# Bucketed attention and two MLPs on one core: the product with v queued behind later scores, and low parts of q and V computed by GpSimd

## The chip, the cores and the metric

The kernel runs on one core of a Trainium2 chip. The metric is device time in microseconds (us) of a whole execution: the three timed runs of the kernel before took 835.03, 836.65 and 831.97 us, a median of 835.03. One further execution was recorded by the hardware profiler.

Names of the engines: PE is TensorE's matmul, PEld its weight load, DVE is VectorE, ACT ScalarE, POOL GpSimd. SP is SyncE, which here only issues DMAs; its queue stands in the trace as SPq. L448 is line 448 of the kernel.

## The reference

For 2 x 8 heads of 768 tokens with 64 numbers each, attention is computed among tokens of the same bucket alone. The bucket is the sign pattern of six projections of the token:

```
q_bits = einsum('bhsd,dk->bhsk', q, proj) > 0          # the same for k
mask   = bucket(q_bits)[:, :, :, None] == bucket(k_bits)[:, :, None, :]
scores = where(mask, q @ k.T / sqrt(64), -1e9)
attn   = exp(scores - max(scores)); attn = attn / (sum(attn) + 1e-9)
x      = (attn @ v), heads side by side: 1536 x 512
h = x @ w_in;   x = (h * sigmoid(1.702 h)) @ w_out     # first MLP, 512 -> 2048 -> 512
h = x @ w_in2;  x = (h * sigmoid(h)) @ w_out2          # second MLP, the same sizes
```

q, k, v and proj are float32; the weights of the MLPs arrive as float64 and are turned into float32 pairs on the chip.

## The kernel before

**Precision by pairs.** TensorE multiplies rounded numbers, so an operand is kept as a high part (rounded) and a low part (what the rounding left), and a product is made of three or so matmuls. The helper `natural` (L287) makes the two parts of q and k: VectorE writes the high part, and a subtraction (L293) gives the low part. Which engine does the subtraction is chosen by `LOWG`, one string for each batch: an operand named there goes to GpSimd, others to VectorE. In the first batch only k is named (and only from the third head on); in the second, k, q and v. V has the same split in `v_high` (L381, ScalarE scales V by a power of two and rounds it to f16) and `v_low` (L385): either one VectorE operation that scales and subtracts (L392), or ScalarE scales V in place (L389) and GpSimd subtracts (L390).

**A step of attention.** A step is 128 queries of one head against its 768 keys. A head has six steps, a batch of eight heads 48, both batches 96. In a step:
- `scores` (L395): four matmuls into PSUM, the bucket mask included by way of extra rows in BQ and BK. Two score buffers exist.
- `top` (L419, VectorE, L422): moves the scores out of PSUM and takes the extreme of each row; `exps` (L425, ScalarE, L427): the exponential.
- `p_high` (L430): the high part in f16, by ScalarE (L438) or VectorE (L436); `p_low` (L440, L442): the low part by GpSimd.
- `p_turn` (L444, L448): one DMA transpose, issued by SyncE, turns the parts of two steps. Two buffers `pt` receive it, so the transpose of a pair waits until the product of the pair before the last has read its buffer.
- `av` (L451): 18 matmuls (L460 to L462) of the transposed exponentials with V; `norm` (L465) divides and puts the result into the MLP's input when a group of steps is done.

Beside the steps, `ahead` (L498) prepares the next pair of heads in twelve slots, one for each step: loads of q, k and v (SyncE, each into a single buffer that is free once the low part has been computed from it), splits, turns on TensorE, copies into BQ and BK, and the bucket bits, whose rows SyncE copies into BQ and BK (`rows`, L342).

**Order of the work.** The program is a loop over steps (L559): in turn i of the first batch it emits `scores(i + 2)`, then `av(i - LAG)` with LAG = 3, `top(i + 1)`, `norm`, `ahead`, `exps(i)`, `p_high(i)`, `p_low(i)` and the transpose of the step before. A planner then simulates the engines and puts each engine's instructions into a queue, by readiness and by priority; the place in the program is the priority, moved forward for some tasks by the offsets in `SOONER`. On the chip each queue runs strictly in order. `tc.issue_after(x)` adds an order to that queue: what is emitted under it comes behind x on x's engine. It is no semaphore.

**The rest.** At turn `SWITCH - 1`, the last of the first batch's loop, the first MLP of the first batch starts and shares the engines with the attention of the second batch. The MLP of the second batch and the whole second MLP follow from about 415 us on. The weights are loaded, split on VectorE, ScalarE and GpSimd (L170 to L178) and partly spilled to HBM and read again.

Of the kernel before, what the change touches and what calls it, by code (L numbers as in the profile page):

```python
# [21 lines left out]
def tile_lsh_attention_two_mlps(  # L22
# [13 lines left out]
    V, A, G, T, SP = nc.vector, nc.scalar, nc.gpsimd, nc.tensor, nc.sync  # L36

    B, H, S, D = q.shape
# [4 lines left out]
    NC = S // P  # L43
    HS = S // 2
    HC = NC // 2
    HEADS = B * H
# [13 lines left out]
    QSCALE = -1.0 / math.sqrt(D)  # L60
    assert math.frexp(QSCALE)[0] == -0.5
    NBUF = 3
    LAG = 3
    TUL = 1
    MORE = {'aq': 1, 'ak': 1, 'p': 1, 'hl': 1, 'pt': 0}
    PTB = 2
    EARLY = 0
    WSTART = 38
    WEVERY = 3
    LOWG = ('k', 'kqv')  # L70
    COPY = ('k', 'q')
    FB = 2
    PB = 2
# [5 lines left out]

    SOONER = ({'ahead': 100, 'move': 20, 'load_v': 400, 'evict': 200, 'p_high': 200, 'natural': 800, 'p_turn': 35, 'turn': 100, 'p_low': 75, 'top': 35, 'exps': 75, 'bits': 300, 'norm': 35, 'load': 50, 'signs': 20}, {'scores': 200, 'evict': 50, 'norm': 300, 'av': 400, 'natural': 200, 'gate': 50, 'p_turn': 20, 'load_v': 200, 'load': 20, 'sum': 150, 'move': 20, 'p_high': 150, 'rows': 100, 'p_low': 75, 'bits': 100, 'exps': 20}, {'gate': 300, 'sum': 10, 'weights': 50})  # L80
    RATE = (3.4, 2.85)
    SWITCH = HEADS // 2 * NC + LAG + 1
    RING = 3
    RING2 = 6

# [2 lines left out]
    def sooner(task):  # L88
        n = SOONER[stage[0]].get(task, 0)
        return tc.high_priority(offset=n) if n else nullcontext()  # L90
# [158 lines left out]
    def attention(sp, s1, ps_m, ps_v, ahead_of, setup):  # L249
        nat, st = {}, {}  # L250
# [12 lines left out]
        N = len(steps)  # L263
# [23 lines left out]
        def natural(n, nm):  # L287
            x = nat[n, nm]
            hp, lp = (1, 0) if nm == "q" else (0, 1)
            E = G if nm in LOWG[stage[0]] and n > 1 else V  # L290
            t = sp.tile([P, NC, 2, D], F32R, tag="s" + nm, name="s" + nm, bufs=1)
# [27 lines left out]
        def place(n):  # L319
            return n % (NBUF + 1) if n < H else (n - H) % NBUF  # L320
# [64 lines left out]
        def v_low(pr, j):  # L385
            vs, s = st["v", pr]
            x = nat[pr, "v"][:, j]
            if "v" in LOWG[stage[0]]:
                A.activation(x, x, AF.Copy, scale=s[:, j:j + 1])  # L389
# [5 lines left out]
        def scores(j):  # L395
            n, c = steps[j]
            aq, ak = st["q", n], st["k", n]
            bq, bk = BQ[place(n)], BK[place(n)]
            ps = ahead_of["pool"].tile([P, 2, 512], F32, tag="s", name="pss")
            lq = aq.rearrange("p a b -> p (a b)")[:, c * P:(c + 1) * P]  # L400
            bq = bq[:, c * P:(c + 1) * P]
            for half in range(2):
                o = ps[:, half, 0:HS]
                T.matmul(o, lhsT=lq, rhs=ak[:, half, :], start=True, stop=False)  # L404
                T.matmul(o, lhsT=bq, rhs=bk[:, half * HS:(half + 1) * HS], start=False, stop=True)  # L405
            st["S", j] = ps[:, :, 0:HS]

        count = {}
# [42 lines left out]
        def av(j):  # L451
            (n, c), g = steps[j], group[j]
            vs, s = st["v", n // 2]
            pt = st.pop(("pt", j))
            if j == g[0]:
                st["av", g] = ps_v.tile([P, 512], F32, tag="av", name="pav")
            o = st["av", g][:, c * (D + 1):(c + 1) * (D + 1)]
            for i in range(NC):
                hv, lv = vs[:, n % 2, i, 0:D + 1], vs[:, n % 2, i, D + 1:]
                T.matmul(o, lhsT=pt[:, i], rhs=hv, start=(i == 0), stop=False)  # L460
                T.matmul(o[:, 0:D], lhsT=pt[:, i], rhs=lv, start=False, stop=False)
                T.matmul(o, lhsT=pt[:, NC + i], rhs=hv, start=False, stop=(i == NC - 1))  # L462


        def norm(g):  # L465
            n, c0 = steps[g[0]]
            m = len(g)
            pr, j = divmod(n, 2)
            vs, s = st["v", pr]
            y = st.pop(("av", g))[:, 0:NC * (D + 1)].rearrange("p (c d) -> p c d", c=NC)[:, c0:c0 + m]  # L470
            ri = sp.tile([P, NC, 1], F32, tag="ri", name="ri", bufs=1)[:, 0:m]
            V.tensor_scalar(ri, y[:, :, D:D + 1], EPS, s[:, j:j + 1], op0=ALU.add, op1=ALU.mult)
            V.reciprocal(ri, ri)
            if ("x", pr) not in st:
                st["x", pr] = sp.tile([P, NC, 2, D], F32, tag="xn", name="xn", bufs=1)
            V.tensor_tensor(out=st["x", pr][:, c0:c0 + m, j, :], in0=y[:, :, 0:D],
                            in1=ri.to_broadcast([P, m, D]), op=ALU.mult)
            if j == 1:
                halves = range(c0 // HC, (c0 + m) // HC)
                for half in halves:  # L480
                    x_turn(pr, half)
                for half in halves:
                    x_split(pr, half)
# [14 lines left out]
        def ahead(pr, s):  # L498
            a, b = 2 * pr, 2 * pr + 1
            return {  # L500
                -4: [(natural, a, "k")],
                -3: [(turn, a, "k", 0), (load, b, "k")],
                -2: [(evict, a, "k", 0), (turn, a, "k", 1), (natural, a, "q")],
                -1: [(evict, a, "k", 1), (turn, a, "q", 0), (v_max, pr), (load, b, "q")],
                0: [(evict, a, "q", 0), (turn, a, "q", 1), (natural, b, "k"), (move, a, "k")],
                1: [(evict, a, "q", 1), (turn, b, "k", 0), (load, a + 2, "k")],
                2: [(turn, b, "k", 1), (v_spread, pr), (natural, b, "q"), (move, a, "q")],
                3: [(evict, b, "k", 0), (evict, b, "k", 1), (turn, b, "q", 0), (v_scale, pr), (load, a + 2, "q")],
                4: [(evict, b, "q", 0), (turn, b, "q", 1), (v_high, pr, 0), (move, b, "k")],
                5: [(evict, b, "q", 1), (bits, pr, 0), (v_low, pr, 0)],  # L510
                6: [(signs, pr, 0), (bits, pr, 1), (v_high, pr, 1), (move, b, "q")],
                7: [(signs, pr, 1), (rows, pr), (v_low, pr, 1)],
                8: [(load_v, pr + 1)],
            }.get(s, [])

        def run(fs):
            for f, *a in fs:
                with sooner(f.__name__):
                    f(*a)
# [36 lines left out]
            run(ahead(1, s))  # L556


        for lead, first, last in ((2, 0, N // 2), (1, N // 2, N)):  # L559
            def at(f, j):  # L560
                if first <= j < last:
                    with sooner(f.__name__):
                        f(j)

            for i in range(first - lead, last + LAG + 1):
                if lead == 2:
                    at(scores, i + 2)
                at(av, i - LAG)
                at(top, i + lead - 1)
                m = i - LAG  # L570
                if first <= m < last and m == group[m][-1]:
                    with sooner("norm"):
                        norm(group[m])
                m = i - 2 * (2 - lead)
                if first <= m < last:
                    pr, s = divmod(m, 2 * NC)
                    with sooner("ahead"):
                        if pr + 1 < HEADS // 2:
                            run(ahead(pr + 1, s))
                        if s >= 2 * NC - 4 and pr + 2 < HEADS // 2:  # L580
                            run(ahead(pr + 2, s - 2 * NC))
                at(exps, i)
                at(p_high, i)
                at(p_low, i)
                at(p_turn, i - TUL)
                yield i
                if lead == 1:
                    at(scores, i + 1)
# [107 lines left out]
    with ExitStack() as es:  # L696
# [9 lines left out]
        for i in attention(sp, s1, ps_m, ps_v, ahead_of, lambda: attention_setup(sp, s1, am, ps_m)):  # L706
            if i == -2:
                for _ in range(EARLY):
                    W.fetch()
            if gen is None and i >= WSTART and i % WEVERY == 0 and W.done < 4:  # L710
                W.step()
            if gen is None and i == SWITCH - 1:
                ps_s.close()
                stage[0] = 1
                ahead_of["lead"] = 1
                ahead_of["more"] = {}
                mb = es.enter_context(tc.tile_pool(name="mlpb", bufs=2))
                ahead_of["pool"] = es.enter_context(tc.tile_pool(name="ps_s1", bufs=1, space=PSUM))
                ps_h = es.enter_context(tc.tile_pool(name="ps_h", bufs=2, space=PSUM))
                gen = mlp(0, [0, 1], [[f, f + 1] for f in range(0, NF, 2)], W, mb, ps_h, True, first1)  # L720
            if gen is not None:
                credit += RATE[i >= 3 * HEADS // 4 * NC]
                while credit >= 1.0:
                    credit -= 1.0
                    next(gen, None)
                    background()
# [41 lines left out]
```

## Time and profile before

| | us |
|---|---|
| timed runs, median (lowest to highest) | 835.03 (831.97 to 836.65) |
| profiled execution | 831.93 |
| its span in the trace | 830.1 |
| PE busy in the span | 753.3 (91%) |
| PEld busy | 692.9 (83%) |
| DVE busy | 533.9 (64%) |
| ACT busy | 421.4 (51%) |
| POOL busy | 442.0 (53%) |

Busy time is the time in which an engine has at least one instruction in work. It says nothing of SyncE, whose queue only issues DMAs: its entries are read from the timeline, where the second number is how long an entry occupied the queue (the transfer itself lands later). The shares are means over stages that have different limits; the first batch of attention lies between about 21 and 163 us, and the stretch in which only the MLPs run begins at about 415 us.

### The profile page before, as it was taken

The page shows a single profiled execution, that of the slowest core. Times are in us where ns is not written, and L with a number is a line of the kernel's source. Part 1 is how long each engine was busy: PE and PEld are TensorE (multiplying, and loading weights), DVE is VectorE, ACT ScalarE, POOL GpSimd, SP SyncE. Part 2 cuts the span into 40 slices and gives each one's busy share as a digit, 9 for nine tenths or more (in the row PEclk, how much of TensorE's full clock was granted, in tenths as well). Part 3 has the DMA queues.
Part 4 walks back from the last instruction along what each step waited for, and adds up shares of the span by engine and source line. Part 5 has one row for each costly group of instructions (what it writes and reads, how often), then busy time and mean ns, then how long its engine had stood idle before and what let it go on. Part 6 is the DMA issues. An engine that isn't in the chain of part 4 may idle for free.

```text
span 830.1 us, 13998 instructions
## 1 busy us (share of the span) xinstructions
PE 753.3 (91%) x5384; PEld 692.9 (83%) x5384; DVE 533.9 (64%) x932; ACT 421.4 (51%) x721; POOL 442.0 (53%) x345
## 2 busy tenths in 40 slices
PE   6787787698898998988999999979999999999998
PEld 5677576577797887887999999979999989998996
DVE  8877787988689889779424233899733843422222
ACT  6758656596675666655534232444645433321220
POOL 5656676777777857766733242549534533421120
PEclk9778979599999999999999999999999999999999
DMA  4999999998998979865587421232310400000112
GB/s 117 190 180 193 200 180 223 231 247 238 246 254 231 223 216 226 210 153 109 108 300 261 150 104 49 77 127 95 108 51 21 132 2 1 0 1 1 39 39 76
DMA packets 196270, 116.40 MB, mean 140 GB/s; under 512 B 153318, under 2 KB 175846, under 8 KB 196204
## 3 DMA queue, kind: packets, MB, share of 16 engines
q1 hardware_dynamic: 196044, 115.52, 55.8%
q8 instruction: 42, 0.69, 0.3%
q14 instruction: 24, 0.20, 0.1%
q10 hardware_dynamic: 160, 0.00, 0.0%
HBM read 56.63 MB, written 16.78 MB: 88 GB/s over the span
## 4 chain that ended last, share of the span: by engine, by line
PE 59%; DVE 20%; DMA 10%; ACT 5%; issue 4%; POOL 1%; SPq 1%; DVEq 0%; ACTq 0%; POOLq 0%
PE pso L642 26%; PE psh L608 25%; DMA pt<-hl 6%; DVE f L173 3%; DVE p L422 3%; DVE f L171 3%; DVE f L175 2%; DVE f L172 2%; PE pss L404 2%; PE pss L405 1%; PE psbit L332 1%; POOL hl L442 1%; DMA nk<-in_k_dram 1%; PE pav L460 1%; ACT p L427 1%
## 5 line engine op out<-in xcount | busy, mean ns | idle before, releaser
L619 POOL TENSOR_TENSOR gl<-g,gh 128x384 fp32r<-128x384 f32 x128 | 138.3, 1081 | 201.7 <-ACT gh L618 189.5
L442 POOL TENSOR_TENSOR hl<-p,hl 128x768 f16<-128x768 f32 x96 | 168.0, 1757 | 75.7 <-ACT hl L438 33.2
L608 PE MATMUL psh<-XH,wih 128*128 128x384 f32 x512 | 174.2, 340 | 6.0 <-DVE part L651 3.9
L608 PE MATMUL psh<-XH,wil 128*128 128x384 f32 x512 | 173.0, 338 | 0.0
L608 PE MATMUL psh<-XL,wih 128*128 128x384 f32 x512 | 172.9, 338 | 0.0
L617 DVE TENSOR_TENSOR g<-g,psh 128x384 f32<-128x384 f32 x96 | 52.7, 550 | 116.8 <-ACT g L616 116.7
L651 DVE SCALAR_TENSOR_TENSOR part<-pso,part 128x384 f32<-128x384 f32 (+1 forms) x124 | 72.6, 590 | 83.0 <-PE pso L642 82.8
L427 ACT ACTIVATE p<-p,lo 128x768 f32<-128x768 f32 x96 | 89.7, 937 | 70.4 <-DVE p L422 70.2
L618 ACT CAST gh<-g 128x384 fp32r<-128x384 f32 x128 | 65.5, 512 | 86.7 <-DVE g L617 70.7
L608 PEld LDWEIGHTS psh<-XH,wih 128*128 128x128 f32 x512 | 97.2, 190 | 8.1 <-DVE g L614 2.2
L642 PE MATMUL pso<-gh,woh 128*128 128x384 f32 x256 | 88.6, 352 | 16.9 <-DVE g L614 7.0
L422 DVE TENSOR_SCALAR_CACHE_REDUCE p<-pss 128x768 f32<-128x768 f32 x96 | 90.8, 947 | 14.9 <-PE pss L405 8.6
L608 PEld LDWEIGHTS psh<-XL,wih 128*128 128x128 f32 x512 | 97.2, 190 | 0.6
L608 PEld LDWEIGHTS psh<-XH,wil 128*128 128x128 f32 x512 | 97.2, 190 | 0.0
L616 ACT ACTIVATE g<-psh 128x384 f32<-128x384 f32 x96 | 46.8, 488 | 96.2 <-PE psh L608 95.2
L404 PE MATMUL pss<-ak,aq 128*128 128x384 f32 x192 | 77.4, 404 | 19.7 <-DVE p L422 19.5
L642 PE MATMUL pso<-gl,woh 128*128 128x384 f32 x256 | 86.5, 338 | 0.0
L642 PE MATMUL pso<-gh,wol 128*128 128x384 f32 x256 | 86.5, 338 | 0.0
L460 PE MATMUL pav<-VS,pt 128*128 128x65 f16 x576 | 69.4, 205 | 15.4 <-DMA pt<-hl 13.0
L460 PEld LDWEIGHTS <-pt 128*128 128x128 f16 x576 | 57.4, 105 | 24.1 <-DMA pt<-hl 17.7
L642 PE MATMUL pso<-woh,gh 128*128 128x512 f32 x192 | 74.9, 390 | 0.2 <-ACT gh L618 0.2
L642 PE MATMUL pso<-wol,gh 128*128 128x512 f32 x192 | 75.0, 391 | 0.0
(114 smaller groups left out, 1623.1 us busy)
## 6 DMA issues: line engine op xcount, KB each, us to landing
raw<-in_moe_w_in_dram SPq DMA_DIRECT2D x32, 512.0 KB
raw<-in_moe_w_out_dram SPq DMA_DIRECT2D x32, 512.0 KB
spih<-wih SPq DMA_DIRECT2D x13, 256.0 KB
spil<-wil SPq DMA_DIRECT2D x13, 256.0 KB
spoh<-woh SPq DMA_DIRECT2D x13, 256.0 KB
spol<-wol SPq DMA_DIRECT2D x13, 256.0 KB
wih<-spih SPq DMA_DIRECT2D x13, 256.0 KB
wil<-spil SPq DMA_DIRECT2D x13, 256.0 KB
```

The costliest lines, as they stand in the source:

```text
L404: T.matmul(o, lhsT=lq, rhs=ak[:, half, :], start=True, stop=False)
L422: V.tensor_scalar(p, st.pop(("S", j)), LOW, None, op0=ALU.min, op1=ALU.min, accum_out=lo)
L427: A.activation(p, p, AF.Exp, bias=lo, scale=-1.0)
L442: G.tensor_tensor(out=hl[:, 1], in0=st.pop(("p", j))[0], in1=hl[:, 0], op=ALU.subtract)
L460: T.matmul(o, lhsT=pt[:, i], rhs=hv, start=(i == 0), stop=False)
L608: T.matmul(h, lhsT=a[:, c], rhs=x[t][:, c], start=(n == 0), stop=(n == 3 * NDC - 1))
L616: A.activation(g, h, AF.Sigmoid, scale=beta)
L617: V.tensor_tensor(out=g, in0=g, in1=h, op=ALU.mult)
L618: A.copy(gh[:, f], g)
L619: G.tensor_tensor(out=gl[:, f], in0=g, in1=gh[:, f].bitcast(F32), op=ALU.subtract)
L642: T.matmul(y, lhsT=a, rhs=x, start=(n == 0), stop=(n == 3 * nf - 1))
L651: V.scalar_tensor_tensor(out=acc, in0=y, scalar=scale, in1=acc, op0=ALU.mult, op1=ALU.add)
```

## The change

In the first batch the lag of the product grows from three steps to four, and the product of step j is ordered behind the last matmul of the scores of step j + 6 in TensorE's queue (for steps up to 41; for the later ones the scores six steps on belong to the second batch and are not yet known at that point). In the first batch the low parts of q, from the third head on, and of V go to GpSimd as those of k do, and ScalarE scales V in place for it. The turn in which the first MLP starts follows the lag. The second batch keeps its lag of three.

```diff
-    LAG = 3
+    LAGS = (4, 3)
-    LOWG = ('k', 'kqv')
+    LOWG = ('kqv', 'kqv')
-    SWITCH = HEADS // 2 * NC + LAG + 1
+    SWITCH = HEADS // 2 * NC + LAGS[0] + 1
...
-                T.matmul(o, lhsT=bq, rhs=bk[:, half * HS:(half + 1) * HS], start=False, stop=True)
+                st["did", j] = T.matmul(o, lhsT=bq, rhs=bk[:, half * HS:(half + 1) * HS], start=False, stop=True).ins
...
-            for i in range(NC):
-                hv, lv = vs[:, n % 2, i, 0:D + 1], vs[:, n % 2, i, D + 1:]
-                T.matmul(o, lhsT=pt[:, i], rhs=hv, start=(i == 0), stop=False)
-                T.matmul(o[:, 0:D], lhsT=pt[:, i], rhs=lv, start=False, stop=False)
-                T.matmul(o, lhsT=pt[:, NC + i], rhs=hv, start=False, stop=(i == NC - 1))
+            first = st.get(("did", j + 6)) if j < N // 2 else None
+            with tc.issue_after(first) if first is not None else nullcontext():
+                for i in range(NC):
+                    hv, lv = vs[:, n % 2, i, 0:D + 1], vs[:, n % 2, i, D + 1:]
+                    T.matmul(o, lhsT=pt[:, i], rhs=hv, start=(i == 0), stop=False)
+                    T.matmul(o[:, 0:D], lhsT=pt[:, i], rhs=lv, start=False, stop=False)
+                    T.matmul(o, lhsT=pt[:, NC + i], rhs=hv, start=False, stop=(i == NC - 1))
...
-        for lead, first, last in ((2, 0, N // 2), (1, N // 2, N)):
+        for lead, first, last, LAG in ((2, 0, N // 2, LAGS[0]), (1, N // 2, N, LAGS[1])):
```

## Rows read from the trace of the kernel before

**Rows 1.** By stretch: length, busy us of PE, PEld, DVE, ACT, POOL, clock, DMA.

```profile
21.57:162.59 141.02, 108.49 (x1175) 94.04 (x1176) 115.61 (x212) 95.75 (x139) 93.30 (x59) 0.80 1.01 200
...
415.00:830.00 415.00, 406.00 (x2147) 381.52 (x2145) 193.88 (x301) 148.71 (x291) 160.69 (x142) 1.00 0.24 82
```

**Rows 2.** Timeline of SyncE's queue, one head pair: start, us in the queue, line, DMA.

```profile
21.57 4.58 SPq L448 DMA_TRANSPOSE pt<-hl  x1
...
70.10 0.52 SPq L279 DMA_DIRECT2D nv<-in_v_dram  x1
70.67 0.85 SPq L347 DMA_DIRECT2D BK<-mk  x1
...
72.49 0.74 SPq L347 DMA_DIRECT2D BK<-mk  x1
...
74.07 0.52 SPq L268 DMA_DIRECT2D nq<-in_q_dram  x1
74.73 4.06 SPq L448 DMA_TRANSPOSE pt<-hl  x1
78.83 0.58 SPq L268 DMA_DIRECT2D nk<-in_k_dram  x1
...
88.97 1.23 SPq L316 DMA_DIRECT2D BQ<-aq  x2
...
104.38 0.39 SPq L279 DMA_DIRECT2D nv<-in_v_dram  x1
```

**Rows 3.** All transposes (line 448): count, ns in the queue, minimum/median/maximum.

```profile
L448 SPq DMA_TRANSPOSE pt<-hl x48: 3580/4210/5894, 21.6 to 408.2; - x48
```

**Rows 4.** Timeline of GpSimd: the low parts that two of these transposes need.

```profile
17.10 3.58 POOL L442 TENSOR_TENSOR hl<-p,hl 128x768 f16<-128x768 f32 x2 [2.96 <-ACT hl L438]
...
70.00 3.26 POOL L442 TENSOR_TENSOR hl<-p,hl 128x768 f16<-128x768 f32 x2
```

**Rows 5.** Low parts by line: busy us, mean ns to 165 us; then minimum/median/maximum.

```profile
L392 DVE SCALAR_TENSOR_TENSOR VS<-nv,sv,VS 128x384 f16<-128x384 f32 x10 | 12.4, 1243 | 0.0
L293 DVE TENSOR_TENSOR sq<-nq,sq 128x384 fp32r<-128x384 f32 x11 | 9.9, 901 | 0.1
...
L293 POOL TENSOR_TENSOR sq<-nq,sq x5: 1113/1131/1439, 156.9 to 281.9; 128x384 fp32r<-128x384 f32 x5
...
L390 POOL TENSOR_TENSOR VS<-nv,VS x6: 894/1113/1427, 179.6 to 321.4; 128x384 f16<-128x384 f32 x6
...
L389 ACT ACTIVATE nv<-nv,sv x6: 607/614/641, 178.9 to 319.0; 128x384 f32<-128x384 f32 x6
...
L392 DVE SCALAR_TENSOR_TENSOR VS<-nv,sv,VS x10: 609/1129/2102, 18.1 to 133.5; 128x384 f16<-128x384 f32 x10
```

**Rows 6.** Waits of SyncE's queue, 20 to 150 us: total us, times, longest.

```profile
SPq L268 <- DVE sq L293: 3.2, 3, 2.2
...
SPq L279 <- DVE VS L392: 0.8, 1, 0.8
...
SPq L448 <- PE pav L462: 0.6, 2, 0.3
...
SPq L268 <- POOL hl L442: 0.2, 1, 0.2
```

**Rows 7.** Matmuls by two times: line 405 (two per step), then 460 (six).

```profile
0.00:44.90 44.90, 8.68 (x22) 4.90 (x22) 0.85 0.69 155
...
0.00:130.30 130.30, 32.63 (x86) 18.50 (x86) 0.86 0.89 177
...
0.00:44.90 44.90, 5.01 (x35) 3.98 (x35) 0.85 0.69 155
0.00:130.30 130.30, 26.45 (x204) 21.82 (x204) 0.86 0.89 177
```

**Rows 8.** Timeline at 55 us: a product's last matmul, and SyncE's next transpose.

```profile
55.31 0.24 PE L462 MATMUL pav<-VS,pt 128*128 128x65 f16 x1
...
55.64 4.53 SPq L448 DMA_TRANSPOSE pt<-hl  x1
```

## The prediction

> **What bounds the kernel now.** I read the busy times by stretch first. From 415 us to the end TensorE is busy 406.0 of 415.0 us at full clock: that is the two MLPs, of which the change touches nothing, so whatever the change wins or loses is won or lost earlier and carried through [rows 1]. In the first batch, 21.57 to 162.59 us, no compute engine is full: TensorE 108.5, VectorE 115.6, ScalarE 95.8, GpSimd 93.3 of 141.0 us. Yet the DMA engines show a share of 1.01. So the second view was SyncE's issue queue. One head pair runs there from one load of V (70.10) to the next (104.38), 34.3 us for 12 steps [rows 2]. It holds six transposes of the exponentials; a transpose occupies the queue 4.21 us at the median and never under 3.58 [rows 3]. Six of them are 25.3 us; four row copies at 0.74 to 0.85 are about 3.2 (two shown), V 0.5, two k and two q loads at 0.58 and 0.52 are 2.2, two copies into BQ 1.2: 32.4 of 34.3 us. The queue has no room; the gap before most entries is about 0.1 us.
>
> Is the queue merely waiting inside those 4 us for its data? No: the transpose at 74.73 needs the low parts that GpSimd ended at 70.00 + 3.26 = 73.26, and the first one, at 21.57, needs those that ended at 17.10 + 3.58 = 20.68 [rows 2, 4]. Reading all 24 pairs in the same way, the data stood ready 0.4 to 8.1 us before the transpose began, and five times less than 1.13 us before. So in this batch the order of engines is: SyncE's queue sets the pace, and VectorE, the engine that the change relieves, does not.
>
> **The change part by part.**
>
> *Low parts of q.* Nine subtractions leave VectorE (eleven stand in the rows; the two of the first heads stay): 9 x 0.90 = 8.1 us. GpSimd gets nine of 1.13 us, 10.2 us, by its own rows for the same subtraction in the second batch [rows 5].
>
> *Low parts of V.* Ten operations of 1.24 us leave VectorE, 12.4 us. ScalarE gets ten scalings of 0.61 us (6.1 us), GpSimd ten subtractions of 1.11 us (11.1 us) [rows 5]. Busy time in the first batch then becomes: VectorE 115.6 - 20.5 = 95; GpSimd 93.3 + 21.3 = 115 of 141; ScalarE 95.8 + 6.1 = 102. All still under the queue's load.
>
> What of it lies on the path? VectorE's relief counts only where SyncE's queue stands still for VectorE. Between 20 and 150 us that is 3.2 us in three waits of a q load for the low part of q (the buffer is free only after it) and 0.8 us in one wait of the V load for the low part of V [rows 6]. These 4.0 us go. What is late next is the same buffer, now released by GpSimd. The nearest row is the load of k, whose low part is on GpSimd already: over the same stretch the loads lost 0.2 us to GpSimd. The bounds for the eight q and four V releases in this stretch: nothing, or each behind one low part of the exponentials, 12 x 1.7 = 20 us. I take 0.2, the row of the same helper on the same queue.
>
> At the start the two V operations of the first pair come in front of or behind the second low part of the exponentials on GpSimd. In front, the first transpose waits until 20.68 + 2 x 1.11 = 22.9 instead of 21.57: 1.3 us. Behind, nothing, or a gain of up to 1.1 us, since the V load would not hold the transpose back. I take 1.3, because the V operations come earlier in the program. For the other four transposes whose data came less than 1.13 us ahead I take nothing (ends 0 and 4 x 1.1 = 4.4): the additional GpSimd work is one operation in every two and a half steps, and VectorE's relief brings the inputs forward.
>
> The VectorE operations that remain have a price in the rows: the low part of V takes 0.61 us at the least and 2.10 at the most [rows 5]. The Trainium skill (SBUF — State Buffer, "SBUF: two separate sides") says why it may be so: GpSimd and a VectorE operation with two inputs in SBUF, or in a two-port mode, hold a shared port pair exclusively, and the other fully blocks. By that rule 21.3 us more of GpSimd would block what is left on VectorE more often, and part of the 20.5 us comes back as longer copies. That fits the spread of the rows, which do not by themselves show the blocker; if all of it came back the sum would lose its 4.0 us.
>
> *Product with V.* A lag of four steps instead of three moves the 18 matmuls of a step, and with the last step of a group its normalization (three VectorE operations, the turn on TensorE and the split), one step later in the program; no DMA is among them. The queueing order adds no semaphore wait; it fixes only the place in TensorE's queue. Counting matmuls up to a given time gives the place they have now: at 130.3 us, 86 halves of scores are done, steps 0 to 42, and 204 / 6 = 34 steps of product; so the product of step 34 comes behind the scores of step 42, eight later, and that of step 35, which follows it at once, seven. At 44.9 us there are 22 halves, steps 0 to 10, and 35 of 36, steps 0 to 5: step 5 came five behind [rows 7]. Reading the whole first batch so, the products come six to eight steps behind, and step 5 is the only one before step 42 that breaks the new rule. The constraint therefore moves one product behind one step of scores and is inert otherwise; what changes the schedule is the later program place. Price 0; ends from -2 us (a product that waits for its transpose no longer has scores behind it) to the price of the rival below. Cover: the engine has 32 idle us in 141 [rows 1].
>
> *The switch to the second batch* follows the lag and comes one step later in the count, at the same program point. Zero; one step, 141 / 47 = 3.0 us, if it came on the path.
>
> **Sum.** -3.2 - 0.8 + 0.2 + 1.3 = -2.5 us. The profiled execution took 831.93 us (span 830.1 and 1.8 around it), so 829.4 by its clock. The three timed runs have a median of 835.03, 3.1 above that execution; against the median it is 832.5, and I say 832.5.
>
> **The rivals.**
>
> *The producers matter more than the slack tells.* VectorE is the busiest engine of the batch, and each of the freed 20.5 us could shorten the way from scores to transpose. Speaking against it: the data are early at 19 of 24 transposes. All that the queue can still give is its own idle time, 34.3 - 32.4 = 1.9 us per pair, four pairs 7.6, and a better start of some 2 us: 835.0 - 9.6 = 825.4.
>
> *Two buffers for the transposed exponentials (the slower side).* The transpose of pair k + 2 writes the buffer that the product of pair k reads. At 55.64 the transpose began 0.1 us after the product's last matmul ended (55.31 + 0.24) [rows 8]; the queue lost 0.6 us in two such waits up to 150 us [rows 6]. Of the 22 transposes that reuse a buffer, five stand so (at 55.64, 61.24, 109.00, 123.97 and 162.59). If the later place puts each of these products behind one further step of scores, the transpose and everything behind it on SyncE's queue waits: from 5 x 0.9 (four matmuls of scores) = 4.5 up to 5 x 3.0 (a whole step) = 15 us. I take 8, nearer to the lower end, since between transposes the queue makes up some: 843. It decides from the point at which products trail the scores by nine steps or more. Against it: they trail by six to eight now, at or past the new bound.
>
> *GpSimd becomes the last before the transposes.* Its load goes from 66% to 81%. If at each of the five tight places one moved subtraction comes first, and two q loads wait behind one low part of the exponentials, 5 x 1.1 + 2 x 1.7 = 8.9 us are lost against the 4.0 won, +4.9: 840. For: GpSimd is the last producer. Against: the data are mostly 2 us early, and the k subtractions take the same place now.
>
> *The change does not do what it says:* the product's order stays as it is. This is contained in the forecast, which counts nothing for it.
>
> **How the numbers follow.** Half a per cent, 4.2 us, is what a measurement of this kernel can tell from no change. Forecast 0.45 (within 0.33, faster 0.10, slower 0.02); producers 0.25 (faster 0.24, same 0.01); two buffers 0.18 (slower 0.14, same 0.04); GpSimd 0.12 (slower 0.09, same 0.03). Together faster 0.34, same 0.41, slower 0.25. The forecast's own range is 829 to 836. To hold 8 in 10 it reaches to both other sides: 822 (the producers' 825.4 and the 2 us for the product, plus the runs' own spread) to 843.
>
> **What would show it.** VectorE's time from 21.6 to 162.6 should fall to about 95 us and GpSimd's rise to about 115. The transposes should still take about 4.2 us each on the queue and about 32 to 34 us per head pair, with no waits of q loads for VectorE. The place of the products, six to eight steps behind the scores, should not change. The prediction fails if the head pair gets under 31 us, which the queue's own sum forbids; if transposes wait several microseconds for the product or for GpSimd; or if the stretch after the first batch, where I count no change, gets longer or shorter by more than 4 us.

## The result, and the profile after

The changed kernel takes 840.23 us (median of seven runs, 839.04 to 842.70) where the kernel before, run beside it on the same chips, takes 834.52 (seven runs, 831.97 to 836.65): a ratio of 1.0070, interval 1.0049 to 1.0090. It is slower by 0.7%, where I had forecast 832.5 and no change.

The profiled execution of after took 842.70 us (span 840.9), the slowest of its seven, and that of before 831.93, at the lower end. So the traces lie 10.8 us apart where the medians lie 5.7; they are read below for where the time went, and sizes are taken from the timed ratios.

First the stretches of after, in the columns of [rows 1]: the one that before had there, then from the first to the last transpose of the first batch, on to the last product with v, and the rest.

```profile
21.57:162.59 141.02, 104.44 (x1138) 90.85 (x1138) 102.95 (x191) 96.29 (x143) 106.33 (x76) 0.82 0.95 193
...
21.23:167.81 146.58, 109.09 (x1202) 94.30 (x1201) 106.71 (x196) 99.29 (x148) 110.61 (x78) 0.83 0.95 193
...
167.81:427.70 259.89, 226.15 (x1979) 210.41 (x1976) 209.04 (x362) 167.31 (x274) 177.02 (x128) 0.95 0.82 199
...
427.70:840.60 412.90, 404.29 (x2133) 380.12 (x2132) 192.74 (x299) 147.94 (x289) 159.30 (x140) 0.99 0.24 82
```

Before has this in the middle one, from the last transpose of its first batch to the last product:

```profile
162.59:415.10 252.51, 225.41 (x1987) 206.89 (x1988) 205.49 (x361) 164.45 (x272) 176.59 (x126) 0.97 0.86 205
```

The ends of the stretches are the last transpose of the first batch and the last start of a matmul of the product (the second number after "to"), before and after:

```profile
162.59 3.90 SPq L448 DMA_TRANSPOSE pt<-hl  x1
```

```profile
167.81 5.35 SPq L449 DMA_TRANSPOSE pt<-hl  x1
```

```profile
L462 PE MATMUL pav<-VS,pt x576: 190/192/278, 30.0 to 414.9; 128*128 128x65 f16 x192
```

```profile
L466 PE MATMUL pav<-VS,pt x576: 191/192/281, 27.0 to 427.5; 128*128 128x65 f16 x192
```

Of the 10.8 us, the first batch takes 167.81 - 162.59 = 5.2, the second (427.5 - 167.81) - (414.9 - 162.59) = 7.4, and the MLPs behind it give 1.8 back (413.4 us for 415.2). The change edits nothing in the second batch. TensorE's busy time there is the same (225.4 and 226.2 us, at a granted clock of 0.97 and 0.95); its idle time grew from 27.1 to 33.7. What ended that idle time, total us, times and longest, before and then after:

```profile
PE pso L642 <- DVE g L614: 7.0, 5, 2.2
...
PE pss L404 <- DVE p L422: 5.1, 6, 1.8
...
PE pav L460 <- DMA pt<-hl: 3.4, 6, 1.4
```

```profile
PE pss L405 <- DVE p L423: 11.7, 7, 3.9
...
PE pav L464 <- DMA pt<-hl: 10.3, 6, 2.5
...
PE pso L646 <- DVE g L618: 6.9, 5, 2.1
```

Products stand longer before their transposes, and scores before VectorE's `top`; the MLP (pso) waits as before. 13.5 us more in these two rows is more than the idle time that was added, so other waits went: it is another order, not one new wait.

In the first batch the prediction's own marks read so. SyncE's waits of 20 to 150 us, answering [rows 6] (three of thirteen rows), and all transposes, answering [rows 3]:

```profile
SPq L449 <- PE pav L466: 5.1, 3, 3.5
...
SPq L280 <- POOL sq L294: 1.0, 1, 1.0
...
SPq L269 <- POOL hl L443: 0.3, 1, 0.3
```

```profile
L449 SPq DMA_TRANSPOSE pt<-hl x48: 3560/4281/6037, 21.2 to 420.8; - x48
```

The waits of q and V loads for VectorE's low parts are gone, and a transpose takes 4.28 us at the median (4.21 before). The rows of this view have to be checked against the timeline: they also count an awaited update that comes while the entry is already in the queue. The 3.5 us in the first row belong to the transpose at 35.90, which began within 0.1 us of the entry before it, and the two rows of loads behind GpSimd are of this kind too. Read from the gaps between the entries instead, transposes stood 1.5 us for a product up to 150 us (0.6 before). From the first to the last transpose of the batch the queue stood 7.7 us before (in gaps over 0.1 us), 4.6 of them ahead of loads of q and V and 2.7 ahead of transposes; after, it stood 7.9, of which 7.4 ahead of transposes and none ahead of those loads.

Low parts and VectorE's high part, by line and form up to 170 us, answering [rows 5], and the same high part before, up to 165 us:

```profile
L437 DVE CAST hl<-p 128x768 f16<-128x768 f32 x19 | 21.1, 1109 | 3.3 <-ACT p L428 3.2
...
L294 POOL TENSOR_TENSOR sq<-nq,sq 128x384 fp32r<-128x384 f32 x10 | 10.6, 1059 | 10.1 <-DVE sq L293 7.0 <-DVE sv L379 2.0 <-POOL hl L443 1.1
...
L391 POOL TENSOR_TENSOR VS<-nv,VS 128x384 f16<-128x384 f32 x10 | 10.0, 1000 | 1.6 <-ACT nv L390 1.5
...
L390 ACT ACTIVATE nv<-nv,sv 128x384 f32<-128x384 f32 x10 | 5.8, 603 | 0.0
```

```profile
L436 DVE CAST hl<-p 128x768 f16<-128x768 f32 x19 | 12.9, 679 | 2.1 <-ACT p L427 1.1 <-ACT BK L314 1.0
```

The moved operations cost what was forecast or a tenth less. The same 19 casts of VectorE, which the change doesn't touch, took 8.2 us more.

### The profile page after: what moved, and what is told of

Its sections match the earlier page's. It is cut to its first block, busy times and chain, and to the rows that moved or that the text cites. A ratio compares the mean times of both kernels' runs of the same rounds, so it can differ in the third digit from the quotient of the medians.

```text
span 840.9 us, 14030 instructions
## 1 busy us (share of the span) xinstructions
PE 753.6 (90%) x5384; PEld 696.2 (83%) x5384; DVE 525.4 (62%) x913; ACT 427.4 (51%) x731; POOL 459.3 (55%) x364
## 4 chain that ended last, share of the span: by engine, by line
PE 61%; DVE 13%; DMA 11%; issue 6%; POOL 5%; ACT 3%; SPq 1%; POOLq 0%; DVEq 0%; ACTq 0%
PE pso L646 28%; PE psh L612 26%; DMA pt<-hl 7%; POOL hl L443 3%; DVE p L423 3%; DVE f L172 2%; DVE f L174 2%; DMA raw<-in_moe_w_in_dram 2%; PE pss L405 2%; PE pss L406 1%; DMA nk<-in_k_dram 1%; DVE f L176 1%; PE pav L464 1%; DMA nv<-in_v_dram 1%; PE psbit L333 1%
## 5 line engine op out<-in xcount | busy, mean ns | idle before, releaser
L443 POOL TENSOR_TENSOR hl<-p,hl 128x768 f16<-128x768 f32 x96 | 165.6, 1731 | 64.3 <-ACT hl L439 32.6
L646 PE MATMUL pso<-gh,woh 128*128 128x384 f32 x256 | 90.7, 360 | 15.9 <-DVE g L618 6.9
L646 PE MATMUL pso<-gl,woh 128*128 128x384 f32 x256 | 88.4, 345 | 0.0
L646 PE MATMUL pso<-gh,wol 128*128 128x384 f32 x256 | 88.3, 345 | 0.0
```

Of the source, the lines that this page charges most:

```text
L443: G.tensor_tensor(out=hl[:, 1], in0=st.pop(("p", j))[0], in1=hl[:, 0], op=ALU.subtract)
L646: T.matmul(y, lhsT=a, rhs=x, start=(n == 0), stop=(n == 3 * nf - 1))
```

## The experiments

All ratios are against the kernel before, run beside each version on the same chip.

**One part at a time, and the product's place.** First I held the loss to be the product's place: with the lag of four and the constraint, products come nearer to the scores, and stand before transposes that have not landed. Counted in TensorE's queue over the first batch, the product comes 6.96 steps behind its scores before and 6.52 after (means). The rival was the load moved to GpSimd.

```diff
-    LOWG = ('k', 'kqv')
+    LOWG = ('kqv', 'kqv')          # lows_only: before with this line alone
```


> The kernel before with the low parts of q and V of the first batch on GpSimd alone; lag and queue order of the product as before. Theory G (GpSimd becomes the last producer in front of the transposes): about 840 us, the whole loss of 5.7 us is here. Theory P (in TensorE's planned queue the products stand nearer behind the scores, 6.5 steps in the mean instead of 7.0, so that TensorE waits at a product for its transpose with scores behind it): about 836, since the mean distance in this plan is 6.75.

Measured 837.73, ratio 1.0069 (1.0043 to 1.0095).

```diff
-    LOWG = ('kqv', 'kqv')
+    LOWG = ('k', 'kqv')            # order_only: after without the low parts
```


> The kernel after with the low parts of q and V back on VectorE; the lag of four and the order behind the scores of step j + 6 stay. Theory G: about 834.5, as before. Theory P: about 839 to 840, since the products stand 6.5 steps behind the scores in this plan, as in the changed kernel; TensorE's waits for transposes at a product between 20 and 150 us are 16 us or more against 9.6 before.

Measured 839.92, 1.0098 (1.0080 to 1.0115).

```diff
-            first = st.get(("did", j + 6)) if j < N // 2 else None
+            first = None                     # no_constraint: after, the lag of four stays
```


> The kernel after without the order behind the scores of step j + 6 (lag of four and GpSimd's low parts stay). If the explicit order itself costs (it puts scores between the two products of a pair): about 835 to 837. If the order is inert, as forecast (the mean distance in the plan is 6.52 with it and without it): 840, within 0.3%.

Measured 847.08, 1.0189 (1.0169 to 1.0210).

```diff
-    LAGS = (4, 3)
+    LAGS = (5, 3)                  # behind7, from after
...
-            first = st.get(("did", j + 6)) if j < N // 2 else None
+            first = st.get(("did", j + 7)) if j < N // 2 else None
```


> The kernel after with a lag of five and the product behind the scores of step j + 7: the products stand 7.3 steps behind the scores in this plan. Theory P: 834 or less, the loss is gone, with fewer of TensorE's waits at a product. Theory G: 840, for GpSimd's work is that of the changed kernel. Theory B (two buffers: the later product holds back the transpose that writes its buffer): 843 or more, with waits of the transposes for the product.

Measured 843.62, 1.0142 (1.0120 to 1.0165).

Each part alone costs as much as both together, so their prices don't add. And the place does not decide: without the constraint the distance is 6.52, as in after, and the kernel is 1.2% slower than after; at 7.33 (behind7), more than before's 6.96, it is slower than after too. The theory of the place fell.

**First part and second part apart.** Comparing the queues of before and after showed another difference. Behind the first batch, where the program is word for word the same (5,730 instructions on the five engines), 44% of the 4,074 entries of TensorE's queue stand at another place. The planner simulates on from where the first batch left it, and other readiness gives other choices. So I crossed the two kernels: one's first part, and from the start of the first MLP on every engine's queue in the order that the other kernel's plan has. The work is unchanged, and the edges order queues without a semaphore.

```diff
+    for e, steps in order.items():           # per engine, the other kernel's order from the first MLP on
...
+        for d in steps:
+            at += d
+            x = traced[e][at]
+            if last is not None:             # x behind last in this queue, no wait
+                tc.add_manual_dep(x, last.name, mybir.DependencyInfo(
+                    mybir.DependencyClass.NoSync, mybir.DependencyReason.DATA), reason="second part's order")
+            last = x
```


> The changed kernel, but all instructions from the start of the first MLP on are held, engine by engine, in the order that they had in the plan of the kernel before (order in the queues alone, no waits, no other work). Theory S (of the 5.7 us, most is not in the first batch but in the second: the change altered the planner's order there, and the new order is worse): 833 to 836, the loss all but gone against 832 before. Theory F (the first batch ends some 5 us later and carries everything behind it): 838 to 840.

> The kernel before, with nothing of the change in it, but from the start of the first MLP on held in the order of the changed kernel's plan. Theory S: 836 to 840, most of the loss without any of the change's work. Theory F: 831 to 833, as before.

| first part | second part's order | median us | ratio (interval) |
|---|---|---|---|
| before | before | - | 1 |
| after | before | 834.27 | 1.0025 (1.0009 to 1.0042) |
| before | after | 840.60 | 1.0094 (1.0076 to 1.0113) |
| after | after | 840.23 | 1.0070 (1.0049 to 1.0090) |

The order of the second part alone, over a first batch with none of the change's work in it, costs all that the change costs. The last products of the two crossed kernels, first after/second before and then first before/second after:

```profile
L470 PE MATMUL pav<-VS,pt x576: 191/192/278, 26.4 to 415.7; 128*128 128x65 f16 x192
```

```profile
L466 PE MATMUL pav<-VS,pt x576: 191/192/281, 28.7 to 424.4; 128*128 128x65 f16 x192
```

With after's order it ends at 424.4 though its first batch is before's; with before's order at 415.7 though its first batch is after's. The last transpose of the first batch begins at 166.33 in the first of the two (shown at the end) and here in the second:

```profile
163.97 4.37 SPq L452 DMA_TRANSPOSE pt<-hl  x1
```

So from there to the last product before's order takes 252.3 us behind its own first batch and 249.4 behind after's; after's order takes 259.7 behind its own and 260.4 behind before's. The same cross with each part of the change alone (lows_only's and order_only's first parts, before's second order):

> Low parts of q and V on GpSimd in the first batch, lag as before, and from the start of the first MLP on the order of the kernel before. Theory S (the loss of 5 us that this part of the change showed alone is the planner's order in the second batch): 831 to 834. If GpSimd's work costs itself: 837 as without the held order.

> The lag of four and the product behind the scores of step j + 6 in the first batch, low parts as before, and from the start of the first MLP on the order of the kernel before. Theory S: 831 to 834. If the lag costs itself: 838 to 840 as without the held order.

Measured 832.40, 0.9996 (0.9978 to 1.0014), and 832.41, 0.9997 (0.9980 to 1.0015). With the rest of the queues held, neither part costs or brings anything that can be measured, and neither does the holding itself; the 0.7 and 1.0% of lows_only and order_only were the order behind them.

**What an arbitrary change costs.** Two tweaks of before's priorities with all the work the same:

```diff
-    SOONER = ({..., 'load': 50, 'signs': 20}, ...)
+    SOONER = ({..., 'load': 60, 'signs': 20}, ...)     # load60: the loads of the first batch
...
-    HIGHV = ((5, (2, 4)), (1, ()))
+    HIGHV = ((5, (1, 3)), (1, ()))                     # high13: which two of five high parts VectorE makes
```


> The kernel before with one priority offset of the first batch's planning altered (loads of q and k 60 instead of 50): the same work on the same engines, nearly the same order in the first batch, another order in the second. Theory S in its wide form (the order before is a good draw of the planner, and another draw costs some 4 to 15 us): 836 or more. If only orders that come from the longer lag or from the low parts lose: 832, within 0.3%.

> The kernel before with VectorE rounding the high parts of steps 1 and 3 of each five in the first batch instead of 2 and 4: the same counts of work on every engine, another order in both batches (mean distance between scores and product 6.75 instead of 6.96). Theory S in its wide form: 836 or more. If the work moved to GpSimd or the lag is what costs: 832, within 0.5%.

load60 took 842.49, 1.0123 (1.0096 to 1.0150), high13 834.29, 1.0028 (1.0009 to 1.0046), less than the 836 or more that I expected. load60's trace has the same signs: its last product, and TensorE's waits behind the first batch.

```profile
L462 PE MATMUL pav<-VS,pt x576: 191/192/278, 30.1 to 429.2; 128*128 128x65 f16 x192
```

```profile
PE pav L460 <- DMA pt<-hl: 8.7, 7, 2.8
...
PE pso L642 <- DVE g L614: 8.4, 7, 2.6
...
PE pss L404 <- DVE p L422: 8.2, 6, 2.9
```

How much of load60's loss lies in its first batch was not separated by a cross. Every plan that the planner made anew was slower, by 0.3 to 1.9%. Before's second order is a good draw among those seen here, and each of these changes ahead of it drew again; that every change would is not shown.

**What in the order costs?** In after's second batch the product comes 3.29 steps behind its scores on the mean, in before's 3.42, and its waits for transposes are longer by 7 us. If that is it, products moved back in after's order must help. Runs of product matmuls of the second batch go behind 12 more MLP matmuls in TensorE's queue, where no turn of the result and no other product is in between (first in after's order, then, as a control, in before's); then the same with the three normalization operations of VectorE moved along by four places; then half of both. In these kernels the order is a packed list; it was made so, in short:

```diff
+    order["PE"] = later(order["PE"], runs_of_products, 12)      # after_products_later, before_products_later
+    order["DVE"] = later(order["DVE"], normalizations, 4)       # after_coherent12; coherent6: 6 and 2
```


> The changed kernel with its own order held from the start of the first MLP on, save that on TensorE each run of product matmuls stands behind 12 more matmuls of the MLP (about 2.1 us), where no turn of the result and no other product is in between. Theory T (the second order is worse because TensorE stands at products whose transposes have not landed: 10.3 us of such waits between 168 and 428 us against 3.4 before): the waits fall to about 4 us and the time to 833 to 836. If the waits at products only take the place of others: 838 to 842, the waits move to the scores or the MLP.

> The kernel before with the same shift of the products in its own second order. Theory T: 829 to 833, the 3.4 us of waits at products go. If the order before is a good draw that any shift spoils: 836 or more.

> The changed kernel, its second order held, products behind 12 more matmuls of the MLP on TensorE and the normalization's three operations behind four more operations on VectorE. Theory T (products in front of transposes that have not landed are what the second order costs): 833 to 837, with VectorE's waits at the normalization under 6 us instead of 21. If the queues' orders only fit as a whole: 845 or more.

> The same with half the shift (6 matmuls, two operations). Theory T: 834 to 838. If the orders only fit as a whole: 840 to 848, between the changed kernel and the full shift.

Measured 855.02, 1.0270 (1.0247 to 1.0293); 845.36, 1.0157 (1.0134 to 1.0180); 850.17, 1.0210 (1.0182 to 1.0237); 840.31, 1.0091 (1.0067 to 1.0116). The first one's waits in the second batch:

```profile
PE pss L409 <- DVE p L427: 14.7, 8, 3.5
...
PE pso L650 <- DVE part L659: 10.3, 7, 3.6
...
PE pav L468 <- DMA pt<-hl: 2.7, 3, 2.2
```

```profile
DVE ri L480 <- PE pav L470: 18.7, 9, 4.1
```

The waits for transposes fell from 10.3 to 2.7 us, as they should, and the kernel lost 15 us more: VectorE, whose order had not moved, stood 18.7 us before the normalization of products that came late (2.1 in after), and the next scores waited for VectorE. With the normalization moved along it is still slower than after, or no faster. In the last version, half of both, TensorE's waits in the second batch are:

```profile
PE pss L409 <- DVE p L427: 12.0, 6, 4.3
...
PE pav L468 <- DMA pt<-hl: 3.3, 3, 2.8
```

The wait for transposes is back at before's size and the time is not, so that wait alone is not the cause. The other wait that had grown, of scores for VectorE's `top` (5.1 before, 11.7 in after), is still 12.0, and no version addressed it.

Last, after with only some engines held in before's second order (again in short):

```diff
-    for e, steps in order.items():
+    for e, steps in order.items() if e in held:    # held: TensorE; or VectorE, ScalarE and GpSimd
```


> The changed kernel with TensorE alone held, from the start of the first MLP on, in the order of the kernel before; the planner orders the other engines anew around it. If TensorE's order carries the loss: 833 to 836, as with all engines held (834.3). If the other engines' order does: 838 or more.

> The changed kernel with VectorE, ScalarE and GpSimd held in the order before from the start of the first MLP on, TensorE and SyncE planned anew around it. If TensorE's order carries the loss: 838 or more. If VectorE's, ScalarE's and GpSimd's do: 833 to 836.

TensorE's order alone: 838.76, 1.0067 (1.0043 to 1.0091). VectorE's, ScalarE's and GpSimd's without TensorE's: 846.65, 1.0166 (1.0140 to 1.0191). The first recovers nothing that can be measured, the second is worse than either kernel, and all engines together recover nearly all. So neither TensorE's order nor that of the three other compute engines is enough by itself. SyncE's queue was held in the cross of all engines and planned anew in both of these runs, so whether its order is the missing piece was not tested. I found no single wait or product in which the loss sits, and which feature makes before's order the better one stays open. No version was faster than before.

## Why the prediction was wrong

**The step that failed** is the price of the new plan: "what changes the schedule is the later program place. Price 0", and with it the stretch after the first batch, "where I count no change". All terms of the sum lie in the first batch. I looked for the price in the place of the products there, whereas the planner passed the difference on into all later queues. The second order costs 0.94% (0.76 to 1.13) by itself, some 8 us, the first part 0.25% (0.09 to 0.42), some 2. The prediction named the mark (4 us in the later stretch; in the traces it grew by 5.6 us, and its second batch by 7.4) but gave it no term and no rival: the fault was to treat the later order as given. That nothing is lost in the MLPs behind 415 us held (they gave 1.8 us back).

**SyncE's queue sets the pace of the first batch: held in part.** A head pair was to take 32 to 34 us; over three pairs it is (145.16 - 42.14) / 3 = 34.3 from V load to V load, before (137.00 - 39.16) / 3 = 32.6. Single pairs spread more (27.1, 38.0 and 37.9 us, with five, six and six transposes in them; before 30.9, 34.3 and 32.6, with as many). The pair under 31 us that the prediction excluded is the one with five transposes, for which its sum over six says nothing. The reading that the data stood ready is right, though the 73.26 us taken for the transpose at 74.73 is the end of the later of two low parts in one row; the one it needs ended at 71.6. These are the loads at the ends of that reading, after and then before:

```profile
42.14 0.51 SPq L280 DMA_DIRECT2D nv<-in_v_dram  x1
...
145.16 1.65 SPq L280 DMA_DIRECT2D nv<-in_v_dram  x1
```

```profile
39.16 0.57 SPq L279 DMA_DIRECT2D nv<-in_v_dram  x1
...
137.00 0.59 SPq L279 DMA_DIRECT2D nv<-in_v_dram  x1
```

**The gain of 4.0 us at the loads and the 0.2 and 1.3 against it.** The loads' waits for VectorE went as counted, and the loads did not stand for GpSimd. (The 0.2 was no standing either: that load, at 33.33, began 0.1 us after the entry before it.) At the start GpSimd did not come in front: the first transpose began at 21.2, and the first V load went behind it (26.25 instead of 21.12). At the second transpose it did. GpSimd took V's low part at 25.02, q's at 26.19 and that of a later step first, and the transpose stood 1.5 us for the low part that ended at 30.39:

```profile
26.19 0.99 POOL L294 TENSOR_TENSOR sq<-nq,sq 128x384 fp32r<-128x384 f32 x1
...
27.15 3.24 POOL L443 TENSOR_TENSOR hl<-p,hl 128x768 f16<-128x768 f32 x2
...
28.53 0.40 SPq L269 DMA_DIRECT2D nq<-in_q_dram  x1
...
30.42 3.66 SPq L449 DMA_TRANSPOSE pt<-hl  x1
```

So the gain didn't show as time, since transposes stood on the same queue in place of the loads. Other transposes waited for low parts too, as the rival of GpSimd had it, but there GpSimd itself had waited, here for ScalarE (in brackets: its idle time and what ended it):

```profile
115.11 1.66 POOL L443 TENSOR_TENSOR hl<-p,hl 128x768 f16<-128x768 f32 x1 [5.11 <-ACT hl L439]
...
116.80 3.67 SPq L449 DMA_TRANSPOSE pt<-hl  x1
```

**VectorE's relief was mis-sized.** 115.6 - 20.5 = 95 us was forecast, 102.95 came. Nearly 3 of the missing 8 us could not leave this stretch: three of the 19 operations ran before 21.57 us (q's at 16.46, V's from 18.14), and the eight of q and eight of V inside it took 17.6 us, not 20.5. Most of the rest is the 19 casts, 679 ns each before and 1109 after (7.1 us more within the stretch). The timelines show why. Of the 38 casts of the two kernels, 17 began while GpSimd had at least 0.27 us of an operation still to do (4 before, 13 after), and each of them ended 0.41 to 0.42 us after that operation. The other 21 took 517 to 560 ns. One of each from after; GpSimd's operation beside the second is the one at 115.11 above, which ended at 116.77:

```profile
50.91 0.56 DVE L437 CAST hl<-p 128x768 f16<-128x768 f32 x1
...
115.18 2.00 DVE L437 CAST hl<-p 128x768 f16<-128x768 f32 x1
```

The rule of the Trainium skill that the prediction weighed (SBUF — State Buffer, "SBUF: two separate sides": GpSimd and VectorE block each other on a shared port pair) says this of VectorE's operations with two inputs in SBUF or in a two-port mode, and the trace agrees for this cast; which mode it runs in, no run here shows. How many casts meet an operation, and how much of it is left, decides, and not GpSimd's busy time alone: in the crosses the mean cast took 869 ns with the low parts alone moved (GpSimd busy 107.37 us) and 771 with the order alone changed (92.79 us). GpSimd's rise to 115 us came as 106.3 in that stretch, 110.6 up to the end of the batch.

**The place of the products was not inert.** It should have stayed at six to eight steps. Counted as in [rows 7] up to 130.3 us, after has 80 halves of scores and 204 matmuls of product: 40 steps against 34, where before has 43 against 34. Before's order would have met the constraint nearly everywhere. The constraint is not what moved the place, for without it (no_constraint) the mean distance is the same 6.52. The new plan put scores later. Lines 406 and 464:

```profile
0.00:130.30 130.30, 31.15 (x80) 18.43 (x80) 0.86 0.84 173
```

```profile
0.00:130.30 130.30, 26.45 (x204) 21.33 (x204) 0.86 0.84 173
```

**The rivals.** That producers matter more fell: the low parts alone, with the rest held, give 0.9996. Two buffers (843) and GpSimd (840) named times near the measured one by the wrong mechanism. The waits that they foresaw are there (transposes for products 0.6 to 1.5 us; TensorE's products for transposes 9.6 to 16.8 between 20 and 150 us), but with the second order held, all of the first batch costs 0.25%, some 2 us. The products stood nearer to the scores, not further behind as the two buffers needed. That 840 and 843 lie near the result is luck.

## What to carry to other kernels

Where a planner orders the queues, its order is part of the kernel: an edit early in the program can be paid for in stretches that it doesn't touch, and the price of the redraw (here 0.3 to 1.9%, the edits included) can be many times that of the edit (here 0 to 0.25%). Measure an edit with the rest of the queues held in the old order, and set a neutral tweak of the priorities beside it, before a mechanism is believed. A prediction for such a kernel needs a term for the redraw, on the slow side where the order before is the best one known.

## What the runs showed of the hardware that was not expected

A delay in the first batch was nearly made up later where the queues kept their order. First after/second before has its last transpose of the first batch at 166.33 us, 3.7 later than before, and its last product at 415.7, only 0.8 later:

```profile
166.33 5.57 SPq L453 DMA_TRANSPOSE pt<-hl  x1
```

A cast of VectorE (128x768, f32 to f16) that began while GpSimd was inside an operation did not end before it: it took up to 2.04 us instead of 0.52 to 0.56, and ended 0.41 to 0.42 us after GpSimd's operation in all 17 cases counted above.
